# A Nyström attention and MLP kernel: W2 as plain loads on the one hardware DMA queue, first loads re-ordered, ACT given more of one LayerNorm group, fills counted per step

## The chip, the cores and the metric

The kernel runs on one core of a Trainium2 chip. The metric is the device time of one execution in microseconds (us). Executions come in runs; a run more than 1.5% above the fastest of the same kernel is classed slow. The span of a profile is some 2 us shorter than the time of the same run. Engines: PE is TensorE (PEld its weight loads), DVE VectorE, ACT ScalarE, POOL GpSimd, SP the SyncE, which here only issues DMAs. The granted clock is the share of TensorE's full clock that the profile shows (0.50 is half clock); the DMA share is the mean busy share of the core's 16 DMA engines.

## The reference

Inputs are q, k, v of 8 sequences x 8 heads x 576 x 64 in fp32, a LayerNorm gain and two weight matrices, W1 (512 x 2048) and W2 (2048 x 512). Cut to what matters:

```python
q_lm = q.reshape(B, H, 32, 18, D).mean(axis=3)     # 32 landmarks; k_lm alike
A, Bm, C = sm(q, k_lm), sm(q_lm, k_lm), sm(q_lm, k)
Z = Bm.T / (norm1(Bm) * norminf(Bm) + 1e-6)
for _ in range(6):
    Z = 2 * Z - Z @ Bm @ Z
x = A @ Z @ C @ v                                  # heads joined: 8 x 576 x 512
xn = (x - mean(x)) / sqrt(var(x) + 1e-6) * g
out = x + maximum(xn @ W1, 0) @ W2
```

## The kernel before

Rows of x are cut into 36 blocks of 128, in 9 groups of four. `mlp()` is a generator of small steps of matmuls; `fill(n)` takes n of them between the steps of the attention, so that PE has work while the other engines do the small steps. Sequences 0 and 1 go through `attention`, the others in pairs through `attention2`, whose tiles are cast by POOL and turned (transposed in 32-blocks) by DVE as "jobs".

```python
load_qk(0); load_v(0)
load_qk(1)                          # waits for staging buffers that POOL's v casts free
...                                 # gain, constants
cast_v(0)
for i in range(HID // W1N):
    load_w1(i)                      # 2 x 256 KB each, fp32, SP's queue
load_v(1)

def load_w2(m):                     # four casting DMAs, fp32 -> fp16, issued by POOL
    keep(nc.gpsimd.dma_start(
        out=w2_16[:, m:m + 4, :],
        in_=moe_w_ch2[m * P:(m + 4) * P, :].rearrange("(m p) f -> p m f", p=P)))
...
for i, _ in enumerate(a1):          # second sequence
    fill(5 if i < 8 else 7)
    settle()
    cast_and_load(pairs[0], pairs[1])
    if 3 <= i < 11:
        pairs[0].next_job()         # turning and summing of the next pair, on DVE
...
rates = [0.5, 1.05, 1.05]           # fills per weight of a step
rows = [lambda i: 4 if i < 3 else 9, lambda i: 8, lambda i: 8]
```

The first matmul uses W1 and writes `psh`; ACT turns it into `hT`; the second uses W2 and writes `pso`; DVE makes the output tile `ot` of it. `psn` are the matmuls of the iteration for Z; between two of them stands one DVE instruction on `st`. `psxt` turns a centred block of x for psh; `psb`, `psec` and `psea` are scores, the first of them of the landmarks, which DVE sums (`lmq`, `lmk`).

The softmax here doesn't subtract the row's maximum and nothing guards it: scores larger than these inputs give would overflow.

## Time and profile before

Three runs stood at first: 376.08, 373.76 and 817.54 us. Of the profiled run:

| | |
|---|---|
| span | 370.3 us |
| PE busy | 330.1 us (89%) |
| ACT, DVE, POOL busy | 163.0, 160.1, 121.9 us |
| DMA, first 50 us | 311 GB/s |
| PE waiting for W2 | 11.9 us |

For comparing kernels I use four marks on the timeline: the first psh, the first pso, the first output tile and the first values of the first pair (pscv). The next lines are the timeline of the kernel before, first PE and DVE, then POOL (start and length in us, engine, source line, operation, output<-inputs, shapes, count, and in brackets the idle time before it and what ended that):

```profile
33.97 1.86 PE L73 MATMUL psh<-xnT,w 128*128 128x256 f16 x8 [0.52 <-DVE xnT L67]
...
56.84 1.04 PE L73 MATMUL pso<-w,hT 128*128 128x512 f16 x4
...
75.56 0.75 DVE L67 SCALAR_TENSOR_TENSOR ot<-pso,rstd,xblk 128x512 f32<-128x512 f32 x1 [4.18 <-PE pso L73]
...
98.36 0.20 PE L73 MATMUL pscv<-natv,ecT 32*32 32x65 f16 x2
...
26.65 1.14 POOL L67 CAST nat<-stg 128x1152 f16<-128x1152 f32 x1 [1.94 <-DMA stg<-in_k_dram]
```

From the first pso to its output tile there are 18.7 us; in the full stretch 16 pso take 3.5. Of these 18.7 us, 11.9 are the wait for W2. The last line is the last of the second sequence's q and k, ready at 27.8 us.

### The profile page before, as it was taken

What the parts mean: (1) busy time and instruction counts of PE and PEld (TensorE: products, weight loads), DVE (VectorE), ACT (ScalarE), POOL (GpSimd) and SP (SyncE); (2) the same over time, 40 slices, a digit from 0 to 9 for tenths busy, and PEclk for the clock granted to TensorE, in tenths of its full rate; (3) what the DMA queues carried; (4) which work ended last, traced back from release to release, by engine and by line L of the source; (5) the groups of instructions that cost most, each with busy time, mean ns of one, the idle gap of its engine ahead of it and who ended that gap; (6) DMA issues with size and microseconds to landing.
All of it is one profiled execution on the core that took longest, in us unless ns stands there. A gap on an engine that the chain in (4) does not pass through costs nothing.

```text
span 370.3 us, 8906 instructions
## 1 busy us (share of the span) xinstructions
PE 330.1 (89%) x3818; PEld 168.5 (46%) x3818; DVE 160.1 (43%) x345; ACT 163.0 (44%) x316; POOL 121.9 (33%) x193
## 2 busy tenths in 40 slices
PE   7767893397769989999999999999999999999994
PEld 6544661043324444445444444554454444444442
DVE  3524654087915985615577730222884011011011
ACT  3437761115426158712664584055425614604600
POOL 2339967138835446952703300000221010000000
PEclk9995999589889999999999999999999999999999
DMA  8899999847493725217301210210022022022013
GB/s 292 268 273 361 350 334 265 206 112 231 148 281 117 255 60 146 105 41 188 84 3 28 58 32 2 59 39 20 2 57 58 0 57 58 0 53 64 0 39 76
DMA packets 21336, 44.63 MB, mean 121 GB/s; under 512 B 2864, under 2 KB 9008, under 8 KB 21296
## 3 DMA queue, kind: packets, MB, share of 16 engines
q1 hardware_dynamic: 19184, 41.95, 38.2%
q0 software_dynamic: 2112, 2.10, 3.4%
q8 instruction: 30, 0.49, 0.5%
q14 instruction: 10, 0.08, 0.1%
HBM read 36.70 MB, written 9.44 MB: 125 GB/s over the span
## 4 chain that ended last, share of the span: by engine, by line
PE 65%; DMA 15%; DVE 9%; ACT 4%; POOL 3%; issue 3%; SPq 1%; DVEq 0%
PE psh L73 30%; PE pso L73 26%; DMA w<-in_moe_w_ch_dram 8%; DMA stg<-in_k_dram 4%; DMA stg<-in_v_dram 3%; DVE xblk L67 3%; PE pscv L73 2%; PE psy L73 2%; DVE ot L67 2%; DVE st L67 2%; POOL natv L67 1%; POOL w L67 1%; PE psxt L77 1%; ACT junk L67 1%; PE psn L73 1%
## 5 line engine op out<-in xcount | busy, mean ns | idle before, releaser
L73 PE MATMUL pso<-w,hT 128*128 128x512 f16 x576 | 139.7, 384 | 11.9 <-DMA w<-in_moe_w_ch_dram 11.9
L73 PE MATMUL psh<-xnT,w 128*128 128x512 f16 (+1 forms) x640 | 136.8, 364 | 7.0 <-issue 3.6
L67 ACT ACTIVATE hT<-psh 128x512 f16<-128x512 f32 x144 | 84.6, 597 | 50.6 <-PE psh L73 50.4
L73 PEld LDWEIGHTS <-w 128*128 128x128 f16 x640 | 60.5, 99 | 66.4 <-issue 11.0
L73 PEld LDWEIGHTS <-hT 128*128 128x128 f16 x576 | 54.4, 99 | 68.0 <-issue 14.8
L67 DVE SCALAR_TENSOR_TENSOR ot<-pso,rstd,xblk 128x512 f32<-128x512 f32 x36 | 26.9, 746 | 107.1 <-PE pso L73 107.0
L67 ACT COPY xnT<-psxt 128x512 f16<-128x512 f16 x32 | 18.7, 584 | 69.4 <-PE psxt L77 69.3
L67 POOL CAST nat<-stg 128x1152 f16<-128x1152 f32 x28 | 31.6, 1147 | 12.2 <-DMA stg<-in_k_dram 6.1
L67 DVE TENSOR_TENSOR xblk<-psy,rcpd 128x512 f32<-128x512 f32 (+1 forms) x40 | 27.6, 691 | 3.9 <-POOL w L67 2.3
L67 POOL TENSOR_SCALAR xn<-xblk,mvg 128x512 f16<-128x512 f32 x12 | 8.3, 696 | 57.7 <-ACT junk L67 31.2
L67 DVE SCALAR_TENSOR_TENSOR st<-st,psn 128x384 f16<-128x384 f16 (+3 forms) x30 | 13.6, 454 | 27.7 <-PE psn L73 27.7
L67 POOL TENSOR_SCALAR xn<-xblk,negm 128x512 f16<-128x512 f32 x20 | 13.9, 696 | 32.8 <-PE psxt L77 31.5
L67 ACT ACTIVATE junk<-xblk 128x512 f16<-128x512 f32 x12 | 7.5, 629 | 32.7 <-DVE xblk L67 32.7
L67 POOL CAST natv<-stg 128x1152 f16<-128x1152 f32 x16 | 18.0, 1151 | 9.5 <-DMA stg<-in_v_dram 9.5
L73 PE MATMUL psy<-zcbd,ea 128*128 128x260 f16 (+1 forms) x80 | 17.0, 297 | 3.1 <-ACT ect L67 1.2
L67 POOL TENSOR_SCALAR negm<-mvg 128x1 f32<-128x1 f32 x20 | 3.8, 192 | 45.7 <-PE psy L73 26.8
L67 DVE STREAM_TRANSPOSE xT<-nat 128x576 uint32<-128x576 uint32 x24 | 18.4, 766 | 0.1
L67 DVE RECIPROCAL rcpd<-psy 128x8 f32<-128x8 f32 (+1 forms) x40 | 8.0, 199 | 21.9 <-PE psy L73 21.4
L67 DVE BATCH_NORM_STATS2 st<-xblk 128x6 f32<-128x512 f32 x24 | 16.6, 690 | 0.7
L67 DVE TENSOR_REDUCE lmk<-xT 128x64 f16<-128x1152 f16 x12 | 16.1, 1346 | 0.1
L67 POOL TENSOR_TENSOR asum<-asum 128x256 f32<-128x256 f32 (+2 forms) x30 | 15.0, 501 | 2.4
L77 PE MATMUL psxt<-ident,xn 128*128 128x128 f16 x144 | 14.4, 224 | 0.7 <-ACT xn L67 0.7
(97 smaller groups left out, 249.4 us busy)
## 6 DMA issues: line engine op xcount, KB each, us to landing
stg<-in_q_dram SPq DMA_DIRECT2D x16, 576.0 KB, 4.9
stg<-in_k_dram SPq DMA_DIRECT2D x16, 576.0 KB, 6.9
out_dram<-ot SPq DMA_DIRECT2D x72, 128.0 KB, 2.4
stg<-in_v_dram SPq DMA_DIRECT2D x10, 576.0 KB, 9.0
w1stg<-in_moe_w_ch_dram SPq DMA_DIRECT2D x16, 256.0 KB, 5.8
stg<-in_v_dram SPq DMA_DIRECT2D x12, 288.0 KB, 9.9
w<-in_moe_w_ch_dram POOLq DMA_DIRECT2D x4, 512.0 KB, 23.9
g_sb<-in_moe_g_ln_dram SPq DMA_DIRECT2D x1, 2.0 KB, 4.9
```

The costliest lines, as they stand in the source:

```text
L67: return lambda *args, **kw: keep(getattr(self.engine, op)(*args, **kw))
L73: keep(nc.tensor.matmul(o, l, r, start=start, stop=stop, tile_position=(rb, cb), skip_group_check=(skip or cb != 0)))
L77: keep(nc.tensor.matmul(o, i_, idn, is_transpose=True, tile_position=(0, 0)))
```

## The change

The intent: put every load on SP's queue in the order of need, so that W2 no longer crawls through the software queue; take work off DVE and POOL where they become busy; and count the fills of each step by hand.

```diff
     load_qk(0)
     load_v(0)
-    load_qk(1)
 ...                                  (DVE's casts of sequence 0 are moved up here)
+    load_qk(1)
 ...
-    def load_w2(m):
-        keep(nc.gpsimd.dma_start(out=w2_16[:, m:m + 4, :], in_=...))
+    def fetch_w2():
+        w2_stg = {}
+        for m in range(MCH + 6):
+            if m < MCH:
+                w2_stg[m] = xpool.tile([P, DM], FP32, name="w2stg", tag="xblk")
+                keep(nc.sync.dma_start(out=w2_stg[m][:], in_=moe_w_ch2[ts(m, P), :]))
+            if m >= 6:
+                pool.tensor_copy(out=w2_16[:, m - 6, :], in_=w2_stg.pop(m - 6)[:])
 ...
     def by_act(j):
-        return 4 <= j < 28 and j % 2 == 0
+        return 4 <= j < 8 or 8 <= j < 28 and j % 2 == 0
 ...
+        elif g == 1:
+            later.append(lambda: center_by_act(j))     (mean, centring, squares: three passes)
 ...
-        fill(5 if i < 8 else 7)
+        fill(5 if i < 8 else 6)
 ...
+    for _ in range(3):
+        pairs[0].next_job()
-    rates = [0.5, 1.05, 1.05]
+    counts = [[5, 5, 12, 12, 12, 12, 5, 5, 3, 3, 3, 3, 4] + 3 * [4] + 7 * [9]]
+    counts += 2 * [[12, 12, 21, 21, 21, 17, 12, 12, 9, 8, 9, 8, 11] + 10 * [8]]
-                fill(6)
+                fill(8)                                (between the leftover jobs)
```

Left out: the weights of the yields, the places of warming matmuls and a few fills in the first phase, and a later reading of which blocks are centred at once. For the second and third pair the new counts are nearly what the rates gave; only the first pair's differ.

## The prediction

> **What bounds the kernel now.** I read the page first (the 40 slices), then the windows table, the waits of TensorE, the chain of waits, and last the timeline around the two holes that these showed. The slices of the page:
>
> ```profile
> span 370.3 us, 8906 instructions
> PE   7767893397769989999999999999999999999994
> PEclk9995999589889999999999999999999999999999
> DMA  8899999847493725217301210210022022022013
> ```
>
> A slice is 9.26 us. From slice 16 on TensorE (PE) is full and at full clock: there the kernel is bound by matmuls, and from 282 us on only the MLP is left. So a microsecond that PE doesn't lose early ends the kernel a microsecond sooner; I only have to count lost PE time. The windows table counts it (columns: window, length, busy us and instructions of PE, PEld, DVE, ACT, POOL, granted clock, DMA share, GB/s):
>
> ```profile
> 50.00:60.00 10.00, 8.76 (x111) 5.51 (x109) 5.79 (x10) 5.02 (x9) 7.39 (x9) 1.00 1.10 306
> 60.00:70.00 10.00, 1.60 (x6) 0.38 (x4) 1.29 (x3) 0.00 (x0) 3.23 (x6) 0.68 1.08 264
> 70.00:80.00 10.00, 7.78 (x28) 3.11 (x27) 5.24 (x10) 1.54 (x4) 2.23 (x4) 0.64 0.44 107
> 90.00:100.00 10.00, 6.88 (x159) 3.19 (x157) 9.40 (x20) 3.68 (x7) 8.31 (x13) 0.83 0.37 95
> 100.00:120.00 20.00, 16.40 (x378) 8.00 (x377) 7.68 (x14) 9.27 (x17) 10.01 (x15) 0.91 0.74 220
> ```
>
> After 140 us the table has under 2 us of idle PE but for the last store. Before it, 0 to 140 us hold 106.0 us of busy PE, so 34.0 idle, and some of the busy time is at a low clock. The biggest hole is at 60 to 70. Its owner stands in the waits of PE, the DMA issues, the chain and the timeline:
>
> ```profile
> PE pso L73 <- DMA w<-in_moe_w_ch_dram: 11.9, 3, 8.4
> PE psb L73 <- DVE lmq L67: 2.4, 2, 1.9
> PE psh L73 <- issue: 3.6, 1, 3.6
> w1stg<-in_moe_w_ch_dram SPq DMA_DIRECT2D x16, 256.0 KB, 5.8
> w<-in_moe_w_ch_dram POOLq DMA_DIRECT2D x4, 512.0 KB, 23.9
> 43.39 30.16 DMA w<-in_moe_w_ch_dram
> 73.59 2.29 PE L73 MATMUL pso<-w,hT 128*128 128x512 f16 x5 [2.22 <-DMA w<-in_moe_w_ch_dram]
> 108.67 3.63 PE L73 MATMUL psh<-xnT,w 128*128 128x512 f16 x10 [3.60 <-issue]
> ```
>
> The second matrix W2 comes in four casting DMAs issued by Pool, each 24 us from issue to landing, and the last lands at 73.6 us, while the first matmul on it (pso) was reached at 56.8. That is 11.9 us of waiting. After it five pso take 2.29 us, 458 ns each, against 216 ns in the full stretch (64 in 13.83 us). Smaller holes follow: scores of the third and fourth sequence wait for DVE (2.4 us), and a 3.6 us hole at 105 us that no engine owns.
>
> **What the Trainium skill says.** (1) "DMA: Bandwidth & Descriptors", section "SWDGE vs HWDGE vs iDMA": a DMA that casts can only be issued from GpSimd, and within each DMA engine the software and hardware queues are served in turn. The trace agrees: 24 us for W2's pieces beside a full hardware queue (DMA share 1.08 to 1.11 from 40 to 70 us). A load without a cast may leave the software queue, which is the change. (2) "TensorE: Matmul & The Clock Gate", section "What's actually happening": after an idle window of about 3.4 us the clock is at half. The trace agrees: 458 ns against 216 after holes of 8.4 and 2.2 us, and 363 ns a matmul after the 3.6 us hole. (3) "Runtime: NRT & Kernel Launch", section "Instruction fetch mechanics": engines fetch instructions by a DMA queue in 16 KiB blocks of 256. The page's instruction queue q8 has 30 packets of together 0.49 MB, which fits PE's 7,638 instructions. I take the 3.6 us hole for a late fetch, since DMA share was 1.01 to 1.06 around it; that is a guess.
>
> **The change part by part.**
>
> Bytes first. A q, k or v tile is 0.59 MB; two sequences are 12 of them, 7.08 MB; W1 and W2 are 4.19 MB each, together 15.46 MB. By the windows table the DMAs moved 298, 270, 283, 375 and 330 GB/s in the first five windows of 10 us, mean 311. In the new order all 15.46 MB would be in at 15.46/0.311 = 49.7 us, and the first tile of the next pair (k0) at 51.6.
>
> (a) Second sequence's q and k. Before, their issue waited for Pool's v casts (13.1 us on) and they shared the queue with W1; Pool cast them at 17.3, 20.3, 23.6 and 26.7. Now they wait for DVE's casts of the first sequence (from 5.4 us). After the six first tiles (13.1 us) one lands each 0.59/0.311 = 1.9 us, the last at 20.7, and its 1.15 us cast ends at 21.9 instead of 27.8. The first x block, which waits for W1's scaling behind these casts, moves about 5 us forward too, and the MLP with it: **5 us gained**, for the moment.
>
> (b) W2. Sixteen pieces of 256 KB behind W1 and v, landed by about 50 us, cast by Pool. A 128x1152 cast is 1.15 us and a 128x512 scaling 0.70, so about 0.6 us each, 9.6 us in all, at the pace of landing (0.84 us a piece). The last is ready at some 50.5 us, and PE needs it about 4 us after its first pso. The 11.9 us wait goes, and with it the half clock: 7 matmuls at 68.8 and 73.6 at some 0.24 us too much, and some of the 2.22 us for seven after that (0.7): about **2.4 us**.
>
> (c) The price: the next pair's loads come after W2. Before, Pool had its first tiles from 44 us on, and DVE turned one at 53.1. The program puts that turning between steps of the short iteration (psn) whose results PE waits for. Now k0 lands at 51.6, its cast ends at 53.4 (one W2 cast ahead), the turning (0.77) at 54.1, the step behind it (0.35) at 54.5, so PE's fifth psn runs at 54.6 instead of 55.3. The 5 us of (a) shrink to about 1; pso starts at about 56 instead of 56.8. Sixteen pso with the pieces between need some 4.5 us, so the first output tile comes at 60.5 to 62.5 instead of 75.6: **13 to 15 us**. I take 14.
>
> (d) ACT centres the second group's four blocks. New there: three passes, 0.63+0.19, 0.72, 0.72+0.19 = 2.45 us a block, 9.8 in all, where two blocks cost 1.73 each before, so ACT gains 6.3 us. DVE loses two statistics of 0.87 us, Pool four centrings of 0.69 and two small ones of 0.19. At 60 to 80 us ACT worked 1.5 of 20 us, so this is hidden, and DVE, 9.40 busy of 10 at 90 to 100, is relieved by 1.7.
>
> (e) Fills counted per step; PE's instruction list has the same 7,638 rows, so its work doesn't change, only what stands between waits. The holes from 76 to 140 us (idle 9.8, plus about 2.7 at low clock) are what this can reach. In the new order DVE has about 20 us of work between 54 and 74 us, with 11 of the 14 turnings and sums before the first scores, and PE about 20.5. That is even, so I expect the 2.4 us wait and some 1.2 us waits to shrink, not all holes. I take **3 us**.
>
> Sum: 14 + 3 = 17 off 376.08, so 359; as some of the early 5 us may survive, I say 358.
>
> **The rivals.** First: DMA is the new bound of the first 60 us. If W2 and k0 come 4 us later than by my mean rate (W1's 1 KB runs gave only 283 GB/s at a share of 0.94), DVE's turning waits, PE waits behind it, and the gain falls to about 10 to 12: 364 to 366. For it: one queue must bring 16 MB before PE can go on. Against it: a queue that is never empty should beat my mean, which contains early waits. Second: DVE or Pool take the place of the wait. Pool must cast W2, then eight q and k tiles with sums and four v tiles before the values are multiplied; if these are late PE waits near 75 to 85 us, and gains of (e) turn into 2 to 4 us lost: 361 to 365. Third: the fetch hole of 3.6 us with its 1.8 at half clock stays or doubles where the queue is fuller: plus or minus 5. Fourth, the good case: the early lead survives and the holes to 140 us go: 370.3 less 12 less 2.4 less 5 less 9, so about 347 with the usual few us above the span.
>
> **Range and chances.** The time is 358, the range 349 to 367: the top is the first or second rival, the bottom close to the fourth. Within 2% would need more than 368.6, so a gain of under 7.5 us, which means that over half of a directly measured 11.9 us wait came back elsewhere. Faster 0.93, same 0.06, slower 0.01.
>
> **What would show it right or wrong.** The changed profile should have no pso waiting for DMA of W2 (under 2 us for its casts by Pool), a first output tile at 60 to 63 us, the last q/k cast of the second sequence at about 22, a DMA share near 1 until at least 55 us, DVE's first turning near 53 to 54 with idle PE of some us just before, ACT under 8 of 10 us busy at 60 to 80, and PE full at full clock from about 120. The prediction is wrong if PE waits more than 5 us in a row near 45 to 60 us, for DVE or Pool behind late loads, or if new holes stand at 70 to 100.

## The result

The changed kernel took 351.52 us in the median of four runs (348.78, 349.01, 354.78, 354.04), beside 374.92 for the kernel before. The ratio is 0.932 with a 95% interval of 0.926 to 0.938. A ratio here compares the mean times of fast runs, so it is not quite the ratio of the medians. The two longer runs count as slow (granted clock 0.981 and 0.982, against 0.991 and 0.990).

The page's slices, span 346.7 (a slice is now 8.67 us), and the windows of the table that the prediction showed, with the same columns:

```profile
span 346.7 us, 8948 instructions
...
PE   8875979879889999999999999999999999999994
...
DMA  7999999999982281171012101210130031022023
```
```profile
50.00:60.00 10.00, 8.24 (x67) 4.26 (x68) 9.21 (x16) 3.36 (x8) 8.13 (x8) 1.00 1.03 385
60.00:70.00 10.00, 8.71 (x90) 4.17 (x89) 8.78 (x15) 9.73 (x25) 9.29 (x14) 1.00 1.02 235
70.00:80.00 10.00, 7.44 (x162) 3.77 (x161) 8.30 (x20) 3.28 (x7) 8.91 (x12) 0.83 1.02 390
90.00:100.00 10.00, 8.30 (x170) 3.57 (x167) 6.24 (x12) 6.01 (x11) 9.37 (x14) 1.00 0.88 239
100.00:120.00 20.00, 18.84 (x133) 8.89 (x132) 17.87 (x40) 8.78 (x23) 6.04 (x13) 1.00 0.43 133
```

The 60 to 70 us window, with 1.60 us of busy PE before, now has 8.71; the one at 90 to 100 has 8.30 instead of 6.88, and 100 to 120 has 18.84 instead of 16.40. PE's waits over the whole span, W2's new row among the DMA issues, and the marks on the timeline:

```profile
PE psn L73 <- DVE st L67: 2.7, 2, 2.1
PE psb L73 <- DVE lmq L67: 2.0, 2, 1.2
...
PE pss L73 <- issue: 1.5, 1, 1.5
...
PE psea L73 <- issue: 1.1, 1, 1.1
```
```profile
w2stg<-in_moe_w_ch_dram SPq DMA_DIRECT2D x16, 256.0 KB, 5.2
```
```profile
20.42 1.14 POOL L67 CAST nat<-stg 128x1152 f16<-128x1152 f32 x1 [0.67 <-DMA stg<-in_k_dram]
...
29.22 1.03 PE L73 MATMUL psh<-xnT,w 128*128 128x256 f16 x8 [0.52 <-DVE xnT L67]
...
47.26 1.28 POOL L67 CAST w<-w2stg 128x512 f16<-128x512 f32 x2 [1.04 <-DMA w2stg<-in_moe_w_ch_dram]
...
49.45 1.15 POOL L67 CAST nat<-stg 128x1152 f16<-128x1152 f32 x1 [0.91 <-PE psh L73]
...
50.63 0.78 DVE L67 STREAM_TRANSPOSE xT<-nat 128x576 uint32<-128x576 uint32 x1 [3.49 <-POOL nat L67]
...
51.70 0.26 PE L73 MATMUL psn<-st 32*32 32x96 f16 x8 [2.10 <-DVE st L67]
...
53.84 0.81 PE L73 MATMUL pso<-w,hT 128*128 128x512 f16 x3
...
59.99 0.74 DVE L67 SCALAR_TENSOR_TENSOR ot<-pso,rstd,xblk 128x512 f32<-128x512 f32 x1
...
77.53 0.24 PE L73 MATMUL pscv<-natv,ecT 32*32 32x65 f16 x3
```

No pso waits for anything (its group has 0.0 us of idle time before it). The last W2 casts end at 48.5 us, 5 us before the first pso. DVE's first turning comes at 50.6, after 3.5 us of waiting for POOL, and PE's fifth psn waits 2.1 us for the step behind it. Stage by stage, from the marks:

| stage | before | after | difference |
|---|---|---|---|
| start to first psh | 33.97 | 29.22 | -4.75 |
| to first pso | 22.87 | 24.62 | +1.75 |
| to first output tile | 18.72 | 6.15 | -12.57 |
| to first pscv of the pair | 22.80 | 17.54 | -5.26 |
| to the end | 271.94 | 269.17 | -2.77 |
| sum | 370.3 | 346.7 | -23.6 |

The table holds one profile of each kernel. The pages cut the same 23.6 us in another way: PE's busy time fell from 330.1 to 323.3 us for the same 3,818 matmuls, so 6.8 us are matmuls that ran faster, and 16.8 us are less idle time. A part of the faster matmuls lies before W2 is needed. At 20 to 30 and 30 to 40 us the granted clock was 0.80 and 0.69 before, 1.00 and 1.00 after. In the profiles of the experiments below, it was 0.54 to 0.61 there with the first loads in the old order (w2_alone, order_back) and 0.87 to 0.96 in the new one (w2_back, act_back, counts_back).

### The profile page after: what moved, and what is told of

It is laid out like the page before. It is cut to its first block, busy times and chain, and to the rows that moved or that the text cites. A ratio compares the mean times of both kernels' runs of the same rounds, so it can differ in the third digit from the quotient of the medians.

```text
span 346.7 us, 8948 instructions
## 1 busy us (share of the span) xinstructions
PE 323.3 (93%) x3818; PEld 166.4 (48%) x3818; DVE 158.7 (46%) x341; ACT 168.6 (49%) x328; POOL 125.5 (36%) x199
## 4 chain that ended last, share of the span: by engine, by line
PE 75%; DVE 7%; DMA 7%; ACT 6%; issue 2%; SPq 1%; POOL 0%; DVEq 0%
PE psh L73 35%; PE pso L73 30%; DMA w1stg<-in_moe_w_ch_dram 4%; DMA g_sb<-in_moe_g_ln_dram 3%; PE pscv L73 3%; ACT xn L67 2%; PE psy L73 2%; PE psxt L77 2%; DVE st L67 2%; DVE xblk L67 2%; PE psn L73 1%; DVE xT L67 1%; ACT junk L67 1%; PE psea L73 1%; PE psec L73 1%
## 5 line engine op out<-in xcount | busy, mean ns | idle before, releaser
L73 PE MATMUL pso<-w,hT 128*128 128x512 f16 x576 | 137.6, 381 | 0.0
L73 PE MATMUL psh<-xnT,w 128*128 128x512 f16 (+1 forms) x640 | 133.7, 358 | 2.9 <-DVE xnT L67 1.2
L73 PEld LDWEIGHTS <-w 128*128 128x128 f16 x640 | 59.7, 98 | 60.6 <-issue 2.3
L67 POOL TENSOR_SCALAR xn<-xblk,negm 128x512 f16<-128x512 f32 x18 | 12.5, 694 | 35.2 <-PE psxt L77 34.1
L67 POOL TENSOR_SCALAR xn<-xblk,mvg 128x512 f16<-128x512 f32 x10 | 6.9, 695 | 45.8 <-PE psxt L77 28.3
L67 POOL TENSOR_SCALAR negm<-mvg 128x1 f32<-128x1 f32 x18 | 3.5, 192 | 37.6 <-PE psy L73 23.9
L73 PE MATMUL psy<-zcbd,ea 128*128 128x260 f16 (+1 forms) x80 | 16.0, 277 | 1.2 <-ACT xT L67 0.6
L67 DVE BATCH_NORM_STATS2 st<-xblk 128x6 f32<-128x512 f32 x22 | 15.2, 689 | 0.6
L77 PEld LDWEIGHTS <-xn 128*128 128x128 f16 x144 | 10.9, 99 | 9.1 <-ACT xn L67 2.0
```

Source lines behind the costliest of these rows:

```text
L67: return lambda *args, **kw: keep(getattr(self.engine, op)(*args, **kw))
L73: keep(nc.tensor.matmul(o, l, r, start=start, stop=stop, tile_position=(rb, cb), skip_group_check=(skip or cb != 0)))
L77: keep(nc.tensor.matmul(o, i_, idn, is_transpose=True, tile_position=(0, 0)))
```

## The experiments

All kernels gave correct results. Each row has four runs; ratios are against the kernel before. The changed kernel had 0.932 at first and 0.927 [0.917, 0.936] when run again.

| run | median us | ratio, 95% interval | first pso | first output tile |
|---|---|---|---|---|
| w2_alone | 361.68 | 0.969 [0.963, 0.975] | 57.69 | 62.20 |
| w2_back | 366.24 | 0.980 [0.975, 0.985] | 51.52 | 73.86 |
| order_back | 356.35 | 0.945 [0.937, 0.953] | 58.53 | 64.69 |
| act_back | 349.91 | 0.940 [0.932, 0.948] | 53.30 | 61.00 |
| counts_back | 355.05 | 0.946 [0.938, 0.953] | 53.08 | 59.23 |
| pair_first | 359.45 | 0.959 [0.950, 0.968] | 61.59 | 68.42 |
| k_first | 354.83 | 0.945 [0.937, 0.953] | 55.60 | 62.47 |
| w2_act_queue | 364.37 | 0.971 [0.965, 0.978] | 65.67 | 71.61 |
| again | 351.44 | 0.927 [0.917, 0.936] | 53.31 | 59.47 |
| k_cast_first | 347.01 | 0.926 [0.919, 0.932] | 50.86 | 56.79 |
| fetch_shift | 349.89 | 0.928 [0.920, 0.937] | 54.24 | 60.18 |
| paced_loads | 349.98 | 0.933 [0.927, 0.940] | 51.73 | 57.66 |

The theory: W2's way through the software queue is most of the gain; the order of the first loads gives a few us more; the rest is small waits. The main rival: the order of the loads carries the gain, and W2's way would be hidden behind it.

### W2 alone, and W2 taken back

```diff
 (kernel before)
-    load_w2(0) ... load_w2(12)       (spread over the rows of the first sequence)
+    cast_v(1)
+    fetch_w2()
```

> The kernel before with one part of the change: W2 in sixteen fp32 pieces on the hardware queue behind the second sequence's v, cast by Pool; order of the first loads, ACT's share and the fill counts as before. Theory 1 (the software queue is the cause of most of the gain): the 11.9 us of waiting and its half clock go, some of it comes back as DVE waiting for the next pair's first tile: 357 to 362, no pso waiting for a DMA, first output tile at 61 to 65 us. Rival (the earlier q and k of the second sequence carry the gain, W2 alone only moves the wait to the later loads): 366 to 372.

```diff
 (changed kernel)
-    cast_v(1)
-    fetch_w2()
+    load_w2(0); load_w2(4); load_w2(8)
+    cast_v(1)
+    load_w2(12)
```

> The changed kernel with W2 again as four casting DMAs issued by Pool, all else kept. Theory 1: the wait for W2 returns, PE comes to its first pso some 3 us earlier than in the kernel before and the last piece lands at 66 to 72 us: 360 to 367. Rival (order of loads is the cause, W2's route is hidden by it): 349 to 353.

Both came out as the theory said: 361.7 and 366.2, and the rival's 366 to 372 and 349 to 353 fall. With W2 back, PE reaches its first pso at 51.5 us, before the changed kernel does (53.8), and then loses more than in the kernel before. Its waits:

```profile
PE pso L73 <- DMA w<-in_moe_w_ch_dram: 14.3, 3, 7.3
```

The time at which the loads are issued is not what makes W2 late: here the casting DMAs were issued at 33.4 to 38.0 us instead of 37.3 to 43.4, and PE still waited for the last until 71.4. What these runs do not separate is the software queue from the cast inside the DMA, since W2's plain loads changed both.

So all the other parts together are worth 8 of the some 25 us while W2 is late. W2 alone gives about 12. The two don't add up to the whole. One thing that stands between them is a new wait in the next stage of w2_alone, which the changed kernel doesn't have; a hole of 3.6 us without an owner (see below) is another. PE's waits of w2_alone begin with:

```profile
PE psxt L77 <- POOL xn L67: 3.6, 1, 3.6
```

POOL, now with W2's casts ahead of the pair's, centres the second group too late. This is what the ACT part is for.

### Parts taken back

```diff
 (changed kernel)
     load_v(0)
+    load_qk(1)
 ...
-    load_qk(1)                       (and the casts in their old places)
```

> The changed kernel with the second sequence's q and k loaded where they were before, behind Pool's v casts and mixed with W1. Theory 1: the first psh comes at 33 to 34 us instead of 29.2 and part of the clock is lost at 20 to 40 us; W2 and the next pair land 1 to 3 us later; 352 to 355. Rival (order carries the gain): 360 or more.

The first psh comes at 33.4 us instead of 29.2, and the output tile at 64.7 instead of 60.0: the early lead is lost and not regained. The median is 356.4, just above the range given, but two of the four runs are slow (358.0 and 358.1); the two fast ones, 351.4 and 354.7, have a mean of 353.0, inside it.

```diff
 (changed kernel)
-        return 4 <= j < 8 or 8 <= j < 28 and j % 2 == 0
+        return 4 <= j < 28 and j % 2 == 0
-        elif g == 1:
-            later.append(lambda: center_by_act(j))
```

> The changed kernel with the second group's statistics and centring as before: two blocks' statistics by ACT, two by DVE, all four centred by Pool. Theory 1 (ACT was idle there, so DVE and Pool are relieved at no cost): 349 to 352, 0 to 3 us slower than the changed kernel. Rival (ACT, 9.7 of 10 us busy at 60 to 70 us and in the chain there, has become the wait): 345 to 348, faster.

349.9 us, three runs at 349.4 to 350.0 and one at 354.1, beside 346.5 to 349.6 for the four fast runs of the changed kernel. The intervals of the ratios overlap (0.932 to 0.948, and 0.926 to 0.938), so a gain of the ACT part is not shown. The traces show what was exchanged. With the part taken back, PE waits for POOL's centring:

```profile
PE psxt L77 <- POOL xn L67: 2.5, 1, 2.5
```

With it, that wait is gone, but ACT is 9.73 of 10 us busy at 60 to 70 and the chain of waits runs through its passes from 60 to 69 us. A wait for POOL was swapped for a full ACT.

```diff
 (changed kernel)
-    counts = [[5, 5, 12, 12, 12, 12, 5, 5, 3, 3, 3, 3, 4] + ...
+    counts = [[6, 6, 10, 10, 10, 8, 6, 6, 4, 4, 4, 4, 5] + ...
-        fill(5 if i < 8 else 6)
+        fill(5 if i < 8 else 7)
-    for _ in range(3):
-        pairs[0].next_job()
-                fill(8)
+                fill(6)
```

> The changed kernel with the fills of the kernel before: 6,6,10,10,10,8,6,6,4,4,4,4,5 instead of 5,5,12,12,12,12,5,5,3,3,3,3,4 in the first pair, 7 instead of 6 in the last steps of the second sequence, 6 instead of 8 between the leftover turnings, and no three turnings ahead of the pair. Theory 1 (counts only shift small waits): 350 to 353. Rival (the counts bring the 5 us that PE gains between the first output tile and the first values of the pair): 354 to 357.

355.1 us, in the rival's range. The output tile comes at 59.2 as with the new counts, but the pair's first values at 79.8 instead of 77.5: that stage takes 20.6 us instead of 17.5. The longest wait for DVE's sums before the second scores is 2.6 us where it was 1.2, and PE's 60 to 70 us window has 7.85 busy instead of 8.71. So in these two profiles the counts and the three jobs moved ahead bring about 3 us there. The last stage, 271.4 against 269.2, has holes of 2.1 and 2.2 us without an owner, see below; how much of the 355 belongs to these, a single profile does not tell. The classing adds to the doubt: the four runs of counts_back (353.0 to 355.8) all count as fast because its fastest is 353.0, while runs of the changed kernel of 353.3 to 354.8 were left out as slow.

### Order within the queue

```diff
 (changed kernel)
+    for _ in range(6):               # pair_first: 6; k_first: 2
+        pairs[0].next_load()
     fetch_w2()
```

> The changed kernel with the first six tiles of the next pair (3.5 MB) loaded ahead of W2 instead of behind it, same queue. Theory 1 with order of need: W2 lands some 9.5 us later, at about 57 to 58 us, the first pso (about 51 us then, no DVE wait) waits some 4 to 6 us in pieces, later loads are as before: 351 to 355. Rival (only leaving the software queue matters, order within the queue is hidden): 346 to 349.

> The changed kernel with only the first two tiles of the next pair (1.2 MB, the ones that DVE turns first) ahead of W2. Theory 1: the 2.1 us in which PE waits for DVE behind the late first tile go, W2 lands 3.2 us later at about 52 us, just in time for pso at 51.5: 346.5 to 349. Rival (W2's casts now become the wait, or the 2.1 us come back at the scores): 349 to 352.

In `k_first` four of the six loads stay in their old place. Both were worse than expected, 359.5 and 354.8, and not by the mechanism that I gave. No pso waited for W2. PE's timeline of pair_first, then PE and POOL of k_first:

```profile
58.02 0.35 PE L73 MATMUL psn<-st 32*32 32x96 f16 x8 [7.65 <-DVE st L67]
```
```profile
52.03 0.35 PE L73 MATMUL psn<-st 32*32 32x96 f16 x8 [3.50 <-DVE st L67]
52.31 2.31 PE L73 MATMUL psh<-xnT,w 128*128 128x256 f16 x10
```
```profile
39.12 10.71 POOL L67 CAST w<-w2stg 128x512 f16<-128x512 f32 x16 [2.41 <-DMA w2stg<-in_moe_w_ch_dram]
49.78 7.83 POOL L67 CAST nat<-stg 128x1152 f16<-128x1152 f32 x7
```

The pair's tiles had landed early, but in POOL's program their casts stand behind all sixteen of W2. In pair_first the first of them starts at 55.8 us instead of 49.5, and PE waits 7.65 us for the turning. In k_first it starts at 49.8, only 0.3 us later than in the changed kernel, but PE got to the wait about 1 us earlier, so the wait of 2.1 us that the run should have removed grew to 3.5. What it cost came mostly after it: the granted clock was 0.50 from 52 to 58 us (0.50 from 54 to 64 in pair_first), where it had stayed at 1.00 after the 2.1 us, and ten psh took 2.31 us instead of 1.27. Of the 2.5 us by which the output tile comes later than in the changed kernel, 0.3 are there when PE goes on, the other 2.2 arise at that clock. The next run moves the casts as well:

```diff
 (k_first; the loop over the other loads is at 6 again, so as many loads stay ahead of the casts)
+    for _ in range(2):
+        pairs[0].next_cast()
     fetch_w2()
```

> As k_first (first two tiles of the next pair loaded ahead of W2), but Pool also casts them ahead of W2's casts. Theory (k_first was slow because Pool, in program order, cast these tiles only after all of W2): no wait of psn for DVE above 0.7 us near 50 us, first pso at 51 to 52, output tile at 57.5 to 59.5 us, 346 to 351, that is 1 to 3 us below the changed kernel of the same call. Rival (the delay of W2 by 1.2 MB is what cost in k_first): pso or its W2 casts wait 2 us or more and the time is no better than k_first, 352 to 355.

```profile
36.66 1.15 POOL L67 CAST nat<-stg 128x1152 f16<-128x1152 f32 x1 [0.37 <-DMA stg<-in_k_dram]
38.09 1.15 POOL L67 CAST nat<-stg 128x1152 f16<-128x1152 f32 x1 [0.28 <-DMA stg<-in_k_dram]
...
45.76 3.98 POOL L67 CAST w<-w2stg 128x512 f16<-128x512 f32 x6 [0.42 <-DMA w2stg<-in_moe_w_ch_dram]
```

W2 is ready at 49.7, the first pso runs at 50.9 and the output tile comes at 56.8, 2.7 us before that of the changed kernel in the same call. The waits of psn for DVE sum to 0.6 us. Against `k_first` the result is clear: 346.9 to 349.6 us beside 352.3 to 356.2, and the expectation's rival (W2's delay itself was the cost) falls. Against the changed kernel it is not. The median is 347.0 us against 351.4, but the ratios, 0.926 and 0.927, do not differ. Nor do the traces show a gain at the output tile: of the 2.7 us, 1.15 are there at the first psh already (28.82 against 29.97), which no edit of this run touches; in the ten profiles of kernels that are alike up to there it comes anywhere from 28.4 to 30.9. And in `again`, the second profile of the changed kernel, the psn that waited 2.1 us in the first waits only 0.7 (1.3 in all).

### W2 on ACT's hardware queue

```diff
-                keep(nc.sync.dma_start(out=w2_stg[m][:], in_=moe_w_ch2[ts(m, P), :]))
+                keep(nc.scalar.dma_start(out=w2_stg[m][:], in_=moe_w_ch2[ts(m, P), :]))
```

> The changed kernel with W2's sixteen plain pieces issued by ACT on the second hardware queue instead of SP. Theory (one queue in order of need matters): the next pair's tiles are no longer behind W2 and share the DMA engines with it, W2 lands later, and ACT loses issue time of about 0.4 us a piece, 6 us, and waits for free buffers: 351 to 358. Rival (any hardware queue does): 348 to 350.

364.4 us, slower than expected. ACT's timeline (ACTq are the DMAs that it issues):

```profile
38.64 11.78 ACTq L229 DMA_DIRECT2D w2stg<-in_moe_w_ch_dram  x15
...
50.52 0.21 ACT L67 ACTIVATE psb<-psb 128x64 f32<-128x64 f32 x1 [11.47 <-DMA w2stg<-in_moe_w_ch_dram]
```

The issues wait for free staging buffers, and ACT's own work stands behind them for 11.5 us; PE then waits 11.2 us. The run says that an engine with work to do is a bad place for issues that must wait. It does not settle whether a second hardware queue would do as well on an idle engine.

### The same kernel again, and the holes without an owner

> The changed kernel itself once more, as the base of this call and for the spread of its runs (348.8 to 354.8 us so far). All theories: median 349 to 355, the same holes without an owner in TensorE's list, at rows 704, 2240, 2496 or 2752, which are all 192 more than a multiple of 256; a run with the lower granted clock should show more or longer ones of them.

> The changed kernel with 112 instead of 80 warming matmuls at the start, of 48 instead of 64 columns, so about the same time but 64 rows more in TensorE's list. Theory (holes without an owner are late fetches of the next block of 256 instructions): the holes keep their row numbers, 704, 2240, 2496, 2752, and so move to other instructions: in the values of the pair (pscv) with 69 and 25 left instead of 37 left and the psh behind, and at a psn instead of psea. Rival (they belong to what these instructions do, or to an unseen wait of theirs): they stay at psea with 9 left, pscv with 37 left and that psh. Time as the changed kernel within 3 us.

The runs of `again` were 349.6, 354.8, 346.5 and 353.3; the two longer ones have a clock of 0.979 each. The profile is of the first run, so what the longer ones lose is not seen.

In every trace, PE has a few holes in which it waits for nothing that the profile shows. I counted PE's instruction list (weight loads and matmuls) to the instruction behind each such hole of over 1 us, in the traces of all kernels here: they stand at four places only, rows 704, 2240, 2496 and 2752, each within two rows or so. Each is 192 more than a multiple of 256. The 3.6 us hole of the kernel before is at row 2496. `fetch_shift` puts 64 rows ahead of all that:

```diff
-    warm(80, 64)
+    warm(112, 48)
```

PE's timeline of `again`, with a hole at row 2752, and of `fetch_shift`, with holes at rows 704 and 2496:

```profile
94.03 0.23 PE L73 MATMUL psea<-xT,lmk 32*32 32x64 f16 x9 [1.63 <-issue]
```
```profile
19.01 0.34 PE L73 MATMUL psn<-st 32*32 32x96 f16 x5 [2.20 <-issue]
...
86.70 0.40 PE L73 MATMUL pscv<-natv,ecT 32*32 32x65 f16 x25 [2.72 <-issue]
```

None stands any more at pss, psea or the psh behind the pscv. One stands, as foretold, at a pscv with 25 left (row 2496). The other is at a psn with 5 left: row 704, for which the expectation had named no place. Rows 2240 and 2752 had none in this run, so two of the places foretold were not tested. So the holes belong to the place in the instruction list, with a period of 256, and not to the work. The Trainium skill, "Runtime: NRT & Kernel Launch", section "Instruction fetch mechanics", has instructions fetched by DMA in blocks of 256. Holes with that period are in keeping with late fetches, and the kept traces show the fetches themselves: each run has 30 packets on the instruction queue (q8 of the page; `--dma --window` tells in which stretch), of 16 KB each. In all 14 profiles together there are 29 such holes, and in every one of them the last packet before PE goes on has ended 1.2 to 1.7 us earlier. The 3.6 us hole of the kernel before, from 105.07 to 108.67 us, has its packet from 105.89 to 107.23. So PE stands there until the next block has come. These packets take 0.9 to 1.6 us, and the others no less (0.9 to 2.4). They are late because they start late, from 1.7 us before the hole begins to 0.8 us after; why is not shown.

```diff
 (k_cast_first)
-        cast_and_load(pairs[0], pairs[1])          (second pair loaded at once)
+        cast_and_load(pairs[0], None)
 ...                                                (2 loads a step in steps 1 to 3 of the first pair;
                                                     casts from step 4 and turnings from step 5,
                                                     instead of steps 0 and 1)
```

> k_cast_first with the loads of the second pair spread over the first steps of the first pair instead of following at once. Theory (late fetches come from full DMA queues at 75 to 100 us): the DMA share there falls below 0.8, holes without an owner after 70 us sum to under 1 us instead of 1 to 4 us, 344 to 349. Rival (DVE gets its turnings later and meets the rows of the pair, or the holes don't depend on the load): holes as before or DVE waits of 3 us and more, 350 to 356.

The theory missed and its rival came true. PE's holes remained (1.9, 1.8, 1.6 and 0.2 us), and the time was 350.0. The DMA share did fall, to 0.73 and 0.71 at 60 to 80 us, but the loads then came at 80 to 100 with shares of 0.98 and 0.97; and the hole at 78 us stood where the share was 0.84 to 0.90. DVE also met the rows of the pair later: 19.5 of 20 us busy at 100 to 120, and psy waited 2.3 us for it. Whether full queues make the fetches late stays open.

## Why the prediction was right

The direction, the owner of the big hole and the range were right: 351.5 us lies in 349 to 367, near its lower end. The mechanism was right too; most sizes were missed, and most of them to the same side, too little gain. By its steps:

- **Bytes first**: the rate was too low. The DMAs moved 347 GB/s in the first 50 us, not 311. Fewer pauses explain little of that, since the DMA share only rose from 0.96 to 0.99; the busy DMA engines moved more in the same time, and why is not shown. In the trace the first tile of the pair is cast at 49.5 to 50.6 us, where I had 53.4 for the end.
- **(a)**: right. The last cast of the second sequence ended at 21.6 us (21.9 predicted), the first psh moved by 4.75 us (5 predicted). What this term left out is the clock: the low clock at 20 to 40 us of the kernel before is in no term, though the windows of the trace had it (0.80 and 0.69), and of the 6.8 us by which PE's busy time fell the prediction counted 2.4 in (b) and up to 2.7 in (e).
- **(b)**: right. No wait of pso for W2 and no half clock behind it are left; w2_back brings back 14.3 us of waiting, w2_alone takes it out. POOL's casts took 0.63 us each (0.6 predicted). Two windows show the clock term: 0.68 and 0.64 at 60 to 80 us before, 1.00 and 0.83 after.
- **(c)**: right in kind, too large. DVE's turning did wait for the pair's first tile, and PE did wait behind it, for 2.1 us in one profile and 0.7 in the next of the same kernel. The early lead shrank from 4.75 to 3.0 us at the first pso, where I had let it shrink to 1. The output tile came at 59.99, so 15.6 us earlier; I had said 13 to 15 and taken 14.
- **(d)**: the arithmetic held, the reading did not. I counted ACT's slack as an average of 60 to 80 us of the kernel before, 1.5 of 20 us, a stretch in which it was stalled by W2. In the changed kernel the same work of ACT falls into 60 to 70 us, where it was 9.73 of 10 us busy (I had said under 8) and in the chain. A net gain is not shown, since against the full ACT stands only a 2.5 us wait for POOL that went away.
- **(e)**: this is the term that was mis-sized. I took 3 us for all after the output tile. The two stages gave 5.3 and 2.8, so 8. About 3 us of it are the counts and the jobs moved ahead (`counts_back`, one profile each). Of the last stage, the one long hole of the kernel before (3.6 us and the half clock behind it) became 1.1 us; this part varies from profile to profile.

Of the rivals, the first (DMA bounds the first 60 us) was half true: the share is at about 1.0 from 10 to 90 us, but the queue ran faster than my mean. The second showed in w2_alone, where POOL's centring came 3.6 us late, not in the changed kernel. The third was right to be kept open: the holes remained, smaller in this profile. The guess that the 3.6 us hole is a late fetch holds (the packet in it, above); that the full DMA queues are the reason is not shown.

Three slips change nothing: the fourth rival's sum is 341.9, which with the 2 us between span and time is 344, not 347; 376.08 was the median of three runs with the odd one among them, while the profile is of a run of 372.35; and the page counts 7,636 matmuls and weight loads, not 7,638. Of the signs named, PE full from about 120 us came true (20.00 of 20 us busy at 120 to 140); the output tile (60 to 63 us) and DVE's first turning (53 to 54) came earlier than said, at 60.0 and 50.6.

## What to carry to other kernels

When a matmul waits for a weight that a casting DMA brings through the software queue beside a full hardware queue, load it plain on the hardware queue, in the order in which it is needed, and cast it on an engine that has time: here that took out all of an 11.9 us wait and the half clock behind it. Moving a load earlier is not enough. The in-order engine that casts it must come to it earlier too, and its other casts must not stand ahead: `k_first` took 354.8 us, `k_cast_first` 347.0. A wait can cost more behind its end than in it: after 3.5 us of idle PE, `k_first` ran some 6 us at half clock. And look at the same kernel's second profile before a wait of 2 us is called removed. Judge the slack of an engine in the stage as it will be, not in one that stands still for another reason.

## What the Trainium skill lacked or had wrong

- "DMA: Bandwidth & Descriptors", section "Anatomy of one DMA — SWDGE (gpsimd) path", fits a software-queue DMA as 2.0 us + bytes/436e3; for 0.52 MB that is 3.2 us as an estimate from the page (4.4 for the 1.05 MB read). Beside a full hardware queue the casting pieces, four in flight, took 23.9 us in the median; plain pieces of 256 KB on the hardware queue took 5.2. No page gives the fit under such load.
- The same page's rule on spreading DMAs over SP, ACT and GpSimd (section "Rules for kernel authors") says that it only saves issue time. The rule gives no figure for what it can cost: issues that wait for a buffer held ACT's own work for 11.5 us (w2_act_queue).
- "Runtime: NRT & Kernel Launch", section "Instruction fetch mechanics", calls the cost of a block boundary mostly hidden. At most boundaries it was, but PE had 29 holes of 1.0 to 3.6 us in 14 profiles of 30 fetches each, at four of the boundaries, each ending 1.2 to 1.7 us after the end of a packet of the instruction queue; they moved with the list when 64 rows were put ahead.
